# Attention and a feed-forward layer on one core: a new order of all queues and a new choice of engines for the same operations

## The chip, the cores and the metric

The kernel runs on one core of one Trainium2 chip. The metric is the device time in microseconds of one execution; the lower the better. The engines are TensorE (PE in the profile, its weight loads PEld), VectorE (DVE), ScalarE (ACT), GpSimd (POOL) and SyncE (SP), on whose queue all DMAs are issued.

## What is computed

The reference, cut to what matters:

```python
# q, k, v: (4, 12, 448, 64); w_in: (768, 2048); w_out: (2048, 768)
scores = cap * tanh(q @ k.T / 8 / cap)
attn = exp(scores - max(scores)); attn = attn / (sum(attn) + 1e-9)
x = (attn @ v) as (4 * 448, 768)
r = maximum(x @ w_in, 0)
out = (s * r * r + b) @ w_out
```

The weights come as 64-bit floats.

## The kernel before

The kernel does not run loops in the order in which they are written. A `Plan` first records 2446 operations, each with a number (its place in the recording), the engines that it may run on, and what it reads and writes. Then `emit` walks through the list `ORDER` (lines 120 and following), word by word. A word is an operation's number; a letter behind it chooses the engine, `a` for ScalarE, `d` for DVE, `p` for POOL, and none the first that the operation names. The words of one engine in their order are that engine's queue. Buffers come from pools with a fixed number of slots (`SLOTS`), given out in the order of the list, so the list also sets which operation waits for which buffer. Nothing else sets the order.

The work goes through these stages, which the list weaves together:

- Attention, for each of 4 batches `bb` and 6 pairs of heads `c2`: `load` and `loadv` bring operands; `plain` and `tail` (lines 426 and 432) are float32 products for the scores; `tanh` and `exp` (lines 441 and 445) run on ScalarE over 128x896 values; `add` on DVE or POOL sums the exponentials; `value`, `ends` and `total` (lines 496, 505, 536) are the products with v and with ones. `evac` and `evacs` (lines 479 and 545 on DVE) bring the results out of PSUM, `normal` turns the sums into reciprocals and spreads them through DRAM, `norm` multiplies.
- The weights. Each tile of w_in and w_out arrives as 64-bit floats and is turned into float32 by `last` (DVE, line 636), `expo` (ScalarE, line 641) and `join` (DVE, line 645); w_in is squared (`sq`, line 679 on DVE) for a norm, w_out summed (`csum`). Then each is split into two float16 halves, `_hi` and `_lo` (lines 341 to 343 and 360).
- `x` is split the same way (`x_hi`, `x_lo`).
- The first layer: `m1` for batches 0 and 1, with 448 columns (lines 828 to 830), and for batches 2 and 3 `m1p`, seven products of half size (line 969) that `plus` (DVE, line 931) joins; the products of the second kind use sums of weights, which `qfull`, `qsums`, `q_hi` and `q_lo` (lines 798 to 812) make, `saveq` stores in DRAM (`wq`, line 815) and `loadq` (line 943) reads back, three tiles for a pair of column groups.
- `relu`, `gsq`, `g_hi`, `g_lo`, `less`, `e_hi`, `e_lo`: the square and its two halves, and sums of them.
- The second layer: `m2` for batch 0 (lines 1140 to 1142), and `m2p` for batches 1 to 3, seven products of 224 columns in two halves each (line 1056), joined by `plus`. `load2` and `loadd` read the weights.

The numbers that the text below speaks of:

| number | operation | engine before, after |
|---|---|---|
| 797, 798 | expo and join of w_in tile (0,0) | ScalarE, DVE in both |
| 818, 819 | expo and join of tile (1,1) | ScalarE, DVE |
| 870, 871 | expo and join of tile (3,2) | ScalarE, DVE |
| 1681, 1645 | e_lo of batch 1, groups 7 and 5 | DVE |
| 1375 | qfull of tile (2,1) | POOL before, DVE after |
| 1391, 1392, 1393 | qsums, q_hi and q_lo of tile (3,1) | DVE, ScalarE; q_lo on DVE before, POOL after |
| 318 | tail of batch 1, pairs 4 and 5: the product that waits for the load of pair 5 | TensorE |
| 1394 | saveq of tile (3,1) | SP |
| 1838, 1839, 1840 | loadq of pair 1 for batch 2 | SP |
| 1753, 1754 | loadd of batch 1, pair 2 | SP |
| 1845 | m1p, batch 2, group 2, product 2: the first that needs pair 1's sums | TensorE |

Of the kernel before, what the change touches and what calls it, by code (L numbers as in the profile page):

```python
# [109 lines left out]
FAST = (1, 2, 3)  # L110
LEVEL = (0, 3, 3, 3)
SPLIT = ()
QUICK = (2, 3)
# [10 lines left out]
76 74 72 77 842 862d 822 75 190 819 824 78 815d 85 825d 89 137 820p 54d 826 57 849 853 86 872d 864 90 84 844 118  # L124
889 58 189 894 854 91 92 134 60 843 850 59 827 100d 122 96 87 851p 97 46 845 855 865 856d 123 119 47 846d 98 93
828 135 890 866 138 857 124 896 99d 94 829 867d 891 895 125 109d 873 874 128 61p 875 832d 131 136 876 126 102
129 127 101 905 111 0 892 834d 881d 48 882 906 887d 121 110 305 49 193 143 112 885d 140 910 150 897 144 139 132
151 130 888 145 133 899 194 141 113 877d 886 146 195 838d 142 191 147 199 196 878 883d 879d 148 830d 907 912 911
893d 200 941 197 149 201 152 202 833 103 908 913 155d 203 915 898p 205 104 153 208 164d 198 914d 836d 62 204 901
916 839 192 247 211 206 880 209 106 221d 50 214 207 884 215 154d 909d 216 900 902 217 218 105 249 166 210 222d  # L130
# [12 lines left out]
993 994 984 837 1432 995 998 508 999 1085 977d 509 985 417 990 986 1000 996 505 991 453 456 1001 461 1404a 1087
1003p 440 1090 462 246 982 469d 463 418a 358 421 420 506 1410a 1411p 1092 997 454 992 457 1451 1002 464 349 1412
1413 429 470d 499 514 458 1452d 1478 465 430 1077 1004d 987 1453p 1086 455 431 507 1414 500 1433 589 466 432 467
1078 468 472d 1091 360 1080 502 978 515 603 1008 477a 471d 1009 473d 587 510 503 1010 359 1484 1479 1485 474d
600 1081 1088 1082 1019a 475 1025a 1083 350 1093 1480 1500 1026 1005d 501 504 498 604 520 1095d 1023a 361p 521
1084 1089 295 1481 1021d 303d 601 422 1094 1024 522 1482d 1405d 476a 486a 1415 488 511 434 527d 1015a 517 1016
487 1096p 1006 1454 362 1416d 1017a 351 1013a 1486 605 512 1424 423 433 516 528d 1007 304 352p 1425 1011a 1434a
425 513 1079 1417p 353 1455 1100 1435d 1014 1101 1020 1102 1012 1111d 1022 1426 518 591 606 1112 1018 1117d  # L150
1113d 489 523 1115p 1487 478 519 607 1483d 1107a 1118 237 1114 524 525 535a 1103a 530d 1108 479 424 1427 526
1177 1466 1456 1104 1097d 1116 435d 1109a 1110 1178 531d 592 1490 529d 1436 490 532d 544a 363 1167 1169 1437
1179 480 1168 1428a 1488a 1172 1491 533 593 1438 1457 1439 1182 1458a 594 597 1173 590 1098 1180 645 588 1429p
1181 1174 1492 1184 598 534d 1440a 1493 1170 1183 1171 1175 1467 1187d 1105a 364 595 1185 1176 1418 608 1099
1419 1489p 596 1186 365 599 1442 1459d 1192 1188d 1193 1194 546 1443 1472 1106 1205a 481 602 1441d 436 1473 619d
1420 1460 1203a 536 537 1206 1421 647 1207a 1189d 538 1209a 482 620d 1514 1208 1210 1474 1494a 1195a 609 1444
1204 655 612 372a 370d 613 1201d 1495d 614 622d 1468 1197a 610 1120 1199d 1196 1198 1190 1202 373 368d 1131 492
1461 656 611 426d 661 1445 664 1200 1446a 369 371 615 646 491 366d 539 374a 1469 623d 616 1422a 662 627a 621d
617 483 618 624d 625 1133 1423d 1191 484d 1126 1132 1447d 1121 1027 1496 367 541 665 378 1127 1134 1497 1462 545
547 1128 663 375 1212 648 636d 1470a 1528 1122 626a 1119 493d 1123 1124 637 1129 494 1471p 1463 1464a 657 1136  # L160
638 548 649 650 652 653 1138 1141p 540 376a 1475 1135 1130 1125 1137 667 1465d 651 666 1476a 1139 658 1142p 1140
1146 427 703 705 1524 542p 1510 639 1143d 654 659 1147 680d 640 1511 1148 628 677d 660 543 629 1477d 550 1155a
1156 1149a 1151a 1150 1152 641 1512 1153a 1154 485 630 549 1157p 1525 1158 1161a 1159a 670 1163a 668 669 671
1286 672 710 707 1160 678d 1498 1211 1034 1499 679d 1039 631 1029 1035 1162 377 1041 681d 1164 1036 708 711 1513
1526 642 1030 632 1028 682d 1031 576d 643d 1040 1501a 1037 1515a 1032 1044 1042 704 1046 1521 1043 1038 683 1213
719 712 1049p 1045 1047 684a 1166 709 696 1033 1048 556p 686 633 1215 1165 1054 1055 673 1050p 674 1214 675 1056
676 1061a 1063a 687 720 1051d 735d 713 722 1059a 685a 1057a 1062 1064 634d 694a 1060 695 1216 714 1144 1058 1218
1217 1527 725 1223 715 635 1069p 1145 1071a 688 551d 697 723 1067p 552 721 553 736d 706 1072 698 724 716 1219
1070 717 1220 1228 689 700 1068 1073 738d 1259 728 1517 1518 726 718 1224 1221 727 1519 737d 1230 1225 739d 740d
1065a 741 699 1226 1229 690 691 729 730 1066 1231 742a 1233d 1227 731 1222 701p 1260 1232 732 744 745 1238 1234p  # L170
733 734 743a 1507 754 1261 753 746 1239 1520 644 702 755 1560 692p 1240 1249a 1262 747 1251a 752a 566d 1253a
1247a 1241a 756 749 748 1235d 1250 758 1255a 1252 1522a 1561 1248 1242 554 1243a 1556 1245a 1562 1236 757 1256
1557 1254 1244 750d 1538 1263 1273 1563 759d 1539 1313 1246 1264 1558 1529a 1074 1559 555 1265 1540 1503 1237
1266 1542 760 1690 764p 693 1535 1564p 1258 1530 1276 1267 1268d 1543 1270 1271d 1541 1277 1274 1290 1544 1531
1546d 1052 1592 1567a 1269 1257 1545 1565a 1278 1275 1279 1283 1568d 1566d 1053 1280 1284d 1281d 1547a 1287
1569d 1291 1292 1285 1610 1593 1300 1532 1502 1303 1282 1614 1288 1289 1548d 1293 1570d 1549a 1594 1297 1551d
1571d 1550d 1298d 1572a 1611 1294 1596 1272 1301 1595 1552d 1573d 1295d 1504 1327 1597 1302 1317 1533 1304 1600d
1603a 1612 1574 1598 1305 1599 1553d 1601a 1578 1296 1575 1613 1306 1307 1314 1604d 1615 1602d 1618d 1299 1579
1308d 1505 1506 1310 1554a 1605d 1311d 1318 1315 1616 1555d 1606d 1628 1319 1576 1316 1577 1715 1330 1629 1580
1582d 1581 1320 1534 1583a 1617 1682 1585a 1321 1619a 1324 1584d 1621a 1586d 1587d 1607d 1608a 1322d 1328 1523  # L180
# [51 lines left out]
def attention_moe_kernel(  # L232
# [1048 lines left out]
```

## Time and profile before

| what | us |
|---|---|
| median of 3 runs | 605.57 |
| lowest and highest | 604.0, 606.81 |
| the profiled execution's own time | 606.2 |
| its span, first to last instruction | 604.0 |

One execution of the kernel was recorded by the hardware profiler. Busy time of an engine is the time in which one of its instructions runs; issuing DMAs does not count. Matmuls are pipelined, so a matmul's own duration is longer than the step to the next, and a busy TensorE need not run at its full pace. In the views below an idle time in brackets stands before the instruction that ended it, with what released it.

### The profile page before, as it was taken

Reading aid. Unit: us, or ns where it says so; the run is one execution under the profiler, and the core shown is the slowest. Engines: PE = TensorE matmul, PEld = TensorE weight load, DVE = VectorE, ACT = ScalarE, POOL = GpSimd, SP = SyncE. Lnnn points to the kernel's source line nnn. Section 1 sums busy time; section 2 is a strip of 40 time slices with the busy share of each in tenths; the row PEclk is TensorE's granted clock in tenths of the full one; section 3 lists DMA queues with packets and bytes.
Section 4 is the critical chain, followed back from the end, with each engine's and each line's share of the span. In section 5 each row is a group of like instructions: output and inputs, shape, how many; then the busy total and the mean of one; then the engine's idle time right before and its main releaser. Section 6 shows DMA issues by size and latency. Waiting matters only on the chain.

```text
span 604.0 us, 12457 instructions
## 1 busy us (share of the span) xinstructions
PE 585.6 (97%) x4871; PEld 385.2 (64%) x4871; DVE 504.8 (84%) x1007; ACT 388.9 (64%) x570; POOL 121.9 (20%) x122
## 2 busy tenths in 40 slices
PE   5999999999999999999999999897999999999997
PEld 2332332343444444435555589897999999999997
DVE  1599999999999999999999999998889663577622
ACT  6999989998977997766869673133776114255100
POOL 0034013003211030411000010215242503363200
PEclk9999999999999999999999999998999999999999
DMA  8777665482435466565576787777575556563671
GB/s 322 293 223 256 172 219 167 113 300 71 113 112 184 141 234 219 167 221 184 211 231 237 239 303 248 263 253 260 183 269 208 186 187 198 178 223 137 248 258 62
DMA packets 56698, 125.24 MB, mean 207 GB/s; under 512 B 12736, under 2 KB 28224, under 8 KB 56640
## 3 DMA queue, kind: packets, MB, share of 16 engines
q1 hardware_dynamic: 56640, 124.45, 61.3%
q8 instruction: 38, 0.62, 0.4%
q14 instruction: 20, 0.16, 0.1%
HBM read 99.88 MB, written 24.47 MB: 206 GB/s over the span
## 4 chain that ended last, share of the span: by engine, by line
PE 62%; DVE 24%; ACT 6%; DMA 5%; issue 2%; SPq 0%; DVEq 0%; ACTq 0%
PE bank L1056 19%; PE bank L969 15%; DVE bed L349 7%; PE bank L829 4%; PE bank L828 4%; PE bank L830 4%; PE bank L496 3%; PE bank L426 3%; ACT bed L441 3%; DVE bed L645 2%; PE bank L1140 2%; PE bank L1142 2%; PE bank L1141 2%; DVE w L360 2%; ACT bed L445 2%
## 5 line engine op out<-in xcount | busy, mean ns | idle before, releaser
L349 DVE TENSOR_TENSOR bed<-bed 128x224 f32<-128x224 f32 (+6 forms) x193 | 150.4, 806 | 4.0 <-ACT bed L991 2.1
L1056 PEld LDWEIGHTS <-bed 128*128 128x128 f16 x1512 | 144.7, 98 | 3.5 <-issue 2.8
L350 POOL TENSOR_TENSOR bed<-bed 128x224 f32<-128x224 f32 (+4 forms) x71 | 71.3, 1018 | 291.0 <-DVE bed L349 88.7
L931 DVE SCALAR_TENSOR_TENSOR bed<-bank,arena,bed 128x224 f32<-128x224 f32 (+1 forms) x150 | 75.5, 525 | 63.4 <-PE bank L1056 26.2
L1056 PE MATMUL bank<-gt,bed 128*128 128x224 f16 x864 | 87.8, 259 | 2.5 <-DVE bed L931 2.5
L441 ACT ACTIVATE bed<-bank,arena 128x896 f32<-128x896 f32 x84 | 82.8, 1012 | 11.3 <-PE bank L426 3.9
L445 ACT ACTIVATE bed<-bed,par 128x896 f32<-128x896 f32 x84 | 85.4, 1049 | 0.1
L426 PE MATMUL bank<-bed 64*128 64x448 f32 x288 | 68.1, 584 | 6.7 <-DMA bed<-in_kq 5.0
L829 PE MATMUL bank<-bed,w 128*128 128x448 f16 x192 | 67.9, 353 | 0.0
L828 PE MATMUL bank<-bed,w 128*128 128x448 f16 x192 | 67.5, 351 | 0.0
L830 PE MATMUL bank<-bed,w 128*128 128x448 f16 x192 | 67.2, 350 | 0.0
L1056 PE MATMUL bank<-bed 128*128 128x224 f16 x648 | 66.8, 259 | 0.0
L969 PE MATMUL bank<-bed 128*128 128x224 f16 x576 | 60.9, 263 | 3.3 <-ACT gt L341 2.4
L496 PE MATMUL bank<-bed 128*32 128x448 f32 x576 | 62.2, 544 | 1.1 <-ACT bed L445 1.1
L969 PEld LDWEIGHTS <-bed 128*128 128x128 f16 x576 | 56.1, 99 | 4.8 <-ACT gt L341 2.6
L426 PEld LDWEIGHTS bank<-bed 64*128 64x128 f32 x288 | 24.9, 191 | 45.1 <-ACT bed L441 19.4
L969 PE MATMUL bank<-bed,w 128*128 128x224 f16 x432 | 45.8, 258 | 0.0
L360 DVE SCALAR_TENSOR_TENSOR bed<-bed,arena 128x256 f16<-128x256 f32 (+2 forms) x78 | 44.0, 594 | 0.0
L341 ACT ACTIVATE bed<-bed,arena 128x256 f16<-128x256 f32 (+2 forms) x56 | 30.9, 583 | 17.5 <-POOL bed L350 10.0
L969 PEld LDWEIGHTS <-w 128*128 128x128 f16 x432 | 41.4, 97 | 0.0
L496 PEld LDWEIGHTS bank<-bed 128*32 128x32 f32 x576 | 16.0, 109 | 39.2 <-issue 29.5
L988 ACT ACTIVATE bed<-bed 128x448 f32<-128x448 f32 x32 | 17.8, 568 | 36.1 <-DVE bed L931 36.0
(129 smaller groups left out, 801.7 us busy)
## 6 DMA issues: line engine op xcount, KB each, us to landing
bed<-ws SPq DMA_DIRECT2D x36, 512.0 KB, 4.6
bed<-w SPq DMA_DIRECT2D x30, 512.0 KB, 5.1
bed<-in_w_out SPq DMA_DIRECT2D x24, 512.0 KB, 4.2
bed<-wq SPq DMA_DIRECT2D x24, 512.0 KB, 4.5
bed<-in_kq SPq DMA_DIRECT2D x24, 448.0 KB, 4.4
bed<-in_w_in SPq DMA_DIRECT2D x18, 512.0 KB, 5.3
bed<-in_v SPq DMA_DIRECT2D x24, 256.0 KB, 4.7
w<-bed SPq DMA_DIRECT2D x12, 512.0 KB, 4.6
```

Source lines behind the costliest of these rows:

```text
L349: "DVE": lambda: nc.vector.tensor_tensor(dst(), a(), c(), op),
L350: "POOL": lambda: nc.gpsimd.tensor_tensor(dst(), a(), c(), op),
L426: nc.tensor.matmul(P[kp][:, h, 0:S], a[:, 0, c * 128:(c + 1) * 128], a[:, 1], start=True, stop=True)
L441: ("tanh", bb, c2, c), lambda: nc.scalar.activation(P[ke], P[kp][:, :, 0:S], AF.Tanh, scale=tsc[:, 0:1]),
L445: ("exp", bb, c2, c), lambda: nc.scalar.activation(P[ke], P[ke], AF.Exp, scale=par[:, 0:1]), r=["par"], w=[ke],
L496: nc.tensor.matmul(P[kp[x]][o, 0:S], P[kv[x]][:, c, o], P[kh[x][c]][:, h], start=not x and c == 0, stop=bool(x) and c == NC - 1,)
L828: nc.tensor.matmul(ps[:, 0:S], wh, x[:, 0], start=(c == 0), stop=False)
L829: nc.tensor.matmul(ps[:, 0:S], wh, x[:, 1], start=False, stop=False)
L830: nc.tensor.matmul(ps[:, 0:S], wl, x[:, 0], start=False, stop=(c == NP - 1))
L931: nc.vector.scalar_tensor_tensor(pick(to), ps, sc[:, 0:1], pick(of), ALU.mult, ALU.add)
L969: nc.tensor.matmul(at(), a(c, za), b(c, zb), start=c == 0 and n == 0, stop=c == NC3 - 1 and n == 2)
L1056: nc.tensor.matmul(at(), w(g, zw), b(g, zb), start=g == 0 and x == 0, stop=g == n - 1 and x == 2,)
```

## The change

Three lists are respelled without their spaces, which changes nothing, and `ORDER` is replaced as a whole. Of the 2446 operations 190 run on another engine; DVE has 836 operations in place of 833, ScalarE 573 in place of 569, POOL 106 in place of 113, TensorE (544) and SP (387) the same. The positions of nearly all words differ. The diff, cut to the lines that hold what the text speaks of:

```diff
-FAST = (1, 2, 3)
-LEVEL = (0, 3, 3, 3)
+FAST = (1,2,3)
+LEVEL = (0,3,3,3)
...
-QUICK = (2, 3)
+QUICK = (2,3)
...
 ORDER = """
-8 12 10 18 27 795 868 9 4 796 3 13 800 14 19 28 15 63 11 21 16 805 24 858 33 20 22 870 30 17 23 25 802 34 26 67
-35 2 36 29 797 65 5 806 801 811 40 798 847 816 64 799d 807 31 37 859 68 32 852 38 41 79 869 80 69 81 82 42 813
-83 871 848 818 808 860 809d 812 821 120 45d 70 863 43 39 88 71 95 803 73 44d 66 804p 56 55 823 814 810 817 861
...
-1342 1729 1697 1661p 1662a 1645d 1343d 559a 1749 1739 1743 1684 1663d 1681d 1740 560 568 1346 1344 1752 1355d
...
-763 1370d 1812 585 1392 575 1753 1775 1754 1776 1393d 1779 1359 1772 1781 1780 1764 1767 1770 1792 1813 1816
-1380p 1773 1381 1382 1371 1820 1786 1372 1383d 1814 1364 1379 1787 1788 1394 1790 1840 1815 1818 1838 1839 1789
-1822 1385p 1373p 1817 1791 1819 1793 1823 1843 1844 1821 1957 1384 1374 1796 1826 1395d 1827 1386 1845 1829a
...
+10 3 4 24 25 26 5 8 27 12 28 15 13 21 2 16 30 18 14 795 40 796 9 33 63 800 11 17 65 34 31 22 19 29 805 67 801
+847 20 868 32 806 811 64 70 23 76 41 42 812 35 77 71 869 6 68 120 72 816 69 43 44d 797 36 863 37 56 848 817 79
+38 55 73 66 88 78 80 74 81 798 852 82 39 821 818 118 819 57 83 89 54d 75 58 870 813 871 853 820d 814 807 85 95
...
+580 1679d 1644a 581d 1663d 1694 1730 1680a 1739 1684 1743 1681d 1645d 558 570 1737 1344 1731 1740 1729 561p 1687
...
+1391 1378d 1785 1764 1392 1792 1816 1788 1790 1787 1818 1813 1364 1815 1820 1359 1393p 1817 1844 1822 1794 1789
...
+1798 1394 1768 1771 1825 1383d 1840 1839 1772 1829a 1838 1753 1395d 1797 1769 1828p 1845 1767 1831a 1847 1830d
...
```

## Rows read from the trace of the kernel before

**Rows 1.** The page: each engine's busy time, share and instructions.

```profile
PE 585.6 (97%) x4871; PEld 385.2 (64%) x4871; DVE 504.8 (84%) x1007; ACT 388.9 (64%) x570; POOL 121.9 (20%) x122
```

**Rows 2.** Stretches: length, busy PE, PEld, DVE, ACT, POOL, granted clock, DMA share, GB/s.

```profile
0.00:20.00 20.00, 13.86 (x92) 4.60 (x96) 1.65 (x7) 14.51 (x18) 0.82 (x10) 1.00 0.89 343
20.00:380.00 360.00, 356.91 (x2574) 167.84 (x2565) 350.30 (x712) 296.03 (x415) 56.01 (x40) 1.00 0.62 201
380.00:425.00 45.00, 39.40 (x391) 37.95 (x389) 39.59 (x72) 13.99 (x20) 14.30 (x10) 0.96 0.73 246
425.00:604.00 179.00, 175.46 (x1828) 174.78 (x1825) 113.25 (x218) 64.34 (x119) 50.76 (x62) 1.00 0.56 195
```

**Rows 3.** The timeline: TensorE's last matmuls (start, length, engine, line).

```profile
598.21 2.46 PE L1056 MATMUL bank<-bed 128*128 128x224 f16 x24
```

**Rows 4.** The timeline of ScalarE and DVE in the first 24 us.

```profile
6.95 1.01 ACT L441 ACTIVATE bed<-bank,arena 128x896 f32<-128x896 f32 x1 [3.01 <-PE bank L426]
...
8.94 2.79 ACT L441 ACTIVATE bed<-bank,arena 128x896 f32<-128x896 f32 x3
...
19.17 1.29 ACT L641 ACTIVATE gt<-gt 128x512 f32<-128x512 f32 x2
...
19.91 0.69 DVE L645 SCALAR_TENSOR_TENSOR gt<-gt 128x512 int32<-128x512 int32 x1 [5.05 <-ACT gt L641]
```

**Rows 5.** DVE's groups by line: busy us, mean ns, idle time before.

```profile
L349 DVE TENSOR_TENSOR gt<-bed,gt 128x448 f16<-128x448 f32 x44 | 27.0, 631 | 0.7 <-POOL gt L343 0.6
...
L679 DVE TENSOR_TENSOR bed<-bed 128x512 bf16<-128x512 f32 x13 | 8.8, 682 | 0.1
...
L479 DVE COPY bed<-bank 128x448 f32<-128x448 f32 x13 | 7.9, 615 | 0.1
...
L545 DVE TENSOR_SCALAR bed<-bank,arena 128x448 f32<-128x448 f32 x7 | 4.7, 675 | 0.5 <-PE bank L536 0.5
```

**Rows 6.** POOL's groups by line and shape.

```profile
L350 POOL TENSOR_TENSOR bed<-bed 128x448 f32<-128x448 f32 x8 | 11.8, 1481 | 60.2 <-DMA bed<-zd 49.8 <-DMA bed<-in_v 10.5
L350 POOL TENSOR_TENSOR bed<-bed 128x512 f32<-128x512 f32 x7 | 10.9, 1559 | 45.9 <-DVE bed L645 32.3 <-DMA bed<-in_v 11.4 <-PE bank L426 2.2
...
L350 POOL TENSOR_TENSOR bed<-bed 128x1024 f16<-128x1024 f32 x1 | 2.1, 2134 | 0.0
```

**Rows 7.** DVE's and POOL's work on bed near 380.8 us (ns min/median/max), and POOL's timeline.

```profile
L349 DVE TENSOR_TENSOR bed<-bed x3: 385/1218/2309, 379.4 to 380.9; 128x224 f32<-128x224 f32 x2, 128x1024 f16<-128x1024 f32 x1
...
380.78 2.15 POOL L350 TENSOR_TENSOR bed<-w 128x1024 f32<-128x1024 f16 x1 [11.96 <-DMA bed<-w]
```

**Rows 8.** The chain that ended last, in order of time, and TensorE's timeline from 380 us.

```profile
74.91 4.87 DMA bed<-in_kq
...
385.79 2.46 PE L1056 MATMUL bank<-gt,bed 128*128 128x224 f16 x24 [2.05 <-DVE bed L931]
...
396.17 1.31 PE L1056 MATMUL bank<-gt,bed 128*128 128x224 f16 x12 [0.45 <-DVE bed L931]
...
417.15 0.45 PE L969 MATMUL bank<-bed 128*128 128x224 f16 x3 [2.39 <-ACT gt L341]
418.31 5.00 PE L969 MATMUL bank<-bed 128*128 128x224 f16 x33 [0.71 <-DMA bed<-wq]
```

**Rows 9.** Timelines of DVE, ScalarE and SP, and the chain, near 400 us.

```profile
397.76 0.42 DVE L807 TENSOR_TENSOR bed<-bed 128x256 f32<-128x256 f32 x1
...
403.04 1.22 DVE L349 TENSOR_TENSOR bed<-bed 128x1024 f16<-128x1024 f32 x1
...
401.30 1.05 ACT L810 ACTIVATE bed<-bed 128x1024 f16<-128x1024 f32 x1
...
400.72 3.89 SPq L815 DMA_DIRECT2D wq<-bed  x3
409.65 2.01 SPq L943 DMA_DIRECT2D bed<-wq  x3
...
411.27 6.99 DMA bed<-wq
```

More of the change, by code (lines that the diff above doesn't have):

```diff
@@ L126 @@
[L126 to L130, printed above, removed]
@@ new lines @@
+1207a 378 368a 1447d 620d 1496 622d 1206 1210 1462 1481 1463 611 1203a 1208 369 621d 590 1126 666 537 649 376a
+536 377 1429d 1131 538 650 370d 1482d 655 539 550 623d 615 1128 1492 703 616 1497 651 493d 1528 366a 484d 627a
+624d 656 1464a 1493 1133 652 661 372a 617 618 625 1132 1465d 374a 1494a 1121 1134 1127 670 1204 485 1129 1122
+626a 373 371 1123 541 1136 367 1124 638 629 540 637 1137 648 1130 1138 1141p 1125 705 1510 1139 1511 1483p 639
+1135 1512 662 1140 657 640 1146 556d 653 1142d 1495d 663 1498 636a 654 375 680d 1147 1513 1148 1499 677d 1190
@@ new lines @@
+1061d 1166 696 1527 686 695 706 1051d 737d 688 697 1059a 1057a 698 1064 1062 726 689 1229 1060 727 738d 1213
+1058 739d 1259 1220 1230 1071a 740d 1556 1065a 1215 1214 1072 699 741 1231 1223 729 576d 1221 1066 1069a 742a
+1144 1070 1519 1224 1216 730 691 700 1225 1226 690 745 1222 1145 744 731 1232 701d 746 754 1233p 753 1542 1227
+755 1073 1217 747 1067a 1234p 1235d 1238 756 1529a 743a 1239 1507 1068 1240 1241a 1243a 1245a 692d 1520 644 1260
+748 1247a 1242 554 555 749 1244 1246 1261 757 758 1255a 1249a 1251a 732 1248 733 750d 734 752a 1560 1263 1557
@@ new lines @@
+1252 1250 759d 1264 1074 1262 1256 1558 1265 1561 1503 1266 1559 1522a 1531 1253a 1313 1538 1273 1267 1270 1254
+1268d 1276 1562 1271d 1543 1052 1287 1277 1272 1258 1523 1274 1564d 1563 1565a 1544 1545 1278 1275 1279 1566d
+1567a 1568d 1547a 1290 1539 1280 1569d 1281d 751 1570d 1690 1540 1541 1283 1291 1535 1592 1593 1532 1596 693
+1546p 1282 1284d 1285 1594 1548p 1571p 1595 1597 1300 1288 1516 1303 702 1572a 1549a 1292 1598 1289 1551d 1269
+1257 1600d 1317 1293 1297 1294 1550d 1573d 1314 1236 1298d 1599 1295d 1552d 1304 1305 1578 1533 1504 1237 1603a
@@ new lines @@
+1897 1806p 1898 1860a 1807d 1863d 1389 2050 1397 1398d 1885 1808a 1809d 1901 1886 1883 1861d 1910 1884 1930
+1864p 1903 1865d 1866p 1904 1906 1905 1888a 1908 1907 1909 1867a 1932 1987 1868p 1911 1913 1916 1399 1929 1914
+1889d 1931 1956 1917 1938 1936 1887p 1892d 1890a 1915 1891p 1958 1934 1933 1919a 1940 1935 1937 1893p 1939 1774
+2019 1894d 1967 1997 1918d 1895d 1921p 1941 1920d 1896d 1960 1942 1943 1944 784d 1995 1923d 1961 1963 1962 1965
+1922d 1964 1969 1924p 1971 1945 1966 1925d 765a 1926a 764d 1968 586 1970 1989 1947a 1778 2048 1991 1927d 1988
@@ new lines @@
+1972 1948d 2018 1990 2023 1992 787d 2051 1973 1993 1946d 2060 1974 1994 2066 1999 1975 774d 1949a 1976 1977d
+1980a 1950p 1996 2056 2015 767d 1981d 2069 1998 2001 1978a 2000 2002 766 1951d 1714 2003 2016 788 1952d 2005d
+785a 2024 2004 768 2008d 2049 2006a 2037 2020 1710 2034 2009d 2007d 2028 2070 2053 2010d 2011d 2025 2026 2027
+1979d 2052 2057 2012d 2013a 1982p 775d 1953d 777d 786 2061 778 2114 2014d 2058 2021 2031 2038 1983d 1984d 1985p
+2059 1954a 2143 2022 2062 1955p 1986d 2029 769d 2144 770p 2063 2054 2064 2072 2065 2067 2035 2030 776 2040 779p
@@ L227 @@
+2344p 2384 2406 2392 2395 2399 2374 2286p 2287a 2351 2354 2364 2345d 2402 2346p 2288p 2413 2347p 2365 2355 2414
[3 rows of a table added]
 """
```

162 lines of the change are left out of this document (71 added, 91 removed), and 6 rows, old and new, of the table ORDER.

## The prediction

> **What bounds the kernel now.** The page comes first: TensorE is busy for 585.6 of 604.0 us [rows 1], so a new order of the same work can win little more than what TensorE idles, 18.4 us, and the part of its busy time in which matmuls stand drawn out. The table of engines by stretch comes next [rows 2]; the reader is to see three stages in it. From 20 to 380 us DVE is busy for 350.3 of 360 us, idle 9.7: whatever DVE has queued before the second products sets the end of that stage, and TensorE, though shown busy, runs drawn out (2574 matmuls in 360 us). From 380 to 425 us both have gaps: TensorE 5.6 us, DVE 5.4. From 425 us TensorE is bound by its own work: 1828 matmuls in 175.46 us, 0.096 each, whatever their inputs do; its missing 3.5 us there lie almost wholly behind its last matmul, which ends at 600.67 [rows 3]. DVE is idle there for 66 us. So the end is: DVE's start, plus DVE's work up to the products, plus what is lost from 380 to 425 us, plus some 179 us that no order shortens.
>
> **The change, part by part.** The first two edits only take spaces out of two tuples and cost nothing; the third replaces the list of operations. No operation is added or removed.
>
> *The start of DVE's work.* DVE stands idle until 19.91 us but for some 1.65 us of small work [rows 2, 4], because the first join (798) waits for ScalarE's rescaling of weight tile (0,0) (797): "5.05 <-ACT gt L641". On ScalarE that is the 16th activation in the old list, the 21st in the new one, behind the constant and 19 tanh or exp of 128x896. ScalarE starts them at 6.95 us and three take 2.79 us, each starting some 0.9 after the one before [rows 4], so 797 would start at about 6.95 + 19 x 0.9 = 24.1, and the join 0.74 behind it, as from 19.17 to 19.91 today, at 24.8: 4.9 us later. DVE's next join (819) waits for 818, four exp or tanh further (some 29), and the one behind it (871) for 870, two further (some 31.5); between these two joins DVE has only two short steps. From there its queue has its inputs in hand. So DVE loses between 4.9 us, if the later waits are made good by TensorE having other work, and 7, if each counts whole. I take 5.5, near the single wait that is certain.
>
> *Work moved between DVE, ScalarE and POOL.* Ahead of the last split of j=1 that TensorE waits for (1681 in the old list, 1645 in the new), I counted both lists by kind. DVE loses four evacuations of 0.615, two of 0.675, three squares of 0.682 [rows 5], two column sums, two x_hi and one x_lo, and gains six normalisations (448 columns, near 0.63 by the subtraction of that width in rows 5), three lesx and some single steps: about 3 us less. TensorE has one block of 12 matmuls (1.15 us) less queued ahead of the matching products. Net, DVE comes to this point some 2 us earlier against TensorE. The six evacuations and three squares go to ScalarE, some 6 us by their times on DVE, and a good part of them before 120 us, where ScalarE is as full as DVE. What covers it is that exp and tanh stand earlier against TensorE's products in the new list, and if that cover fails up to 3 us come back; that is in the range.
>
> *POOL.* Ahead of the same point POOL has 34 operations, not 38: six fewer normalisations (1.48 each), two more column sums (1.56), the rest near even [rows 6], some 6 us less. It matters since DVE is drawn out beside POOL: a subtraction of 128x224 that otherwise takes 0.385 took 2.309 us while POOL ran 2.15 us from 380.78 [rows 7]. The bounds are 0 (POOL's operations mostly hit no DVE work) and 6 (each blocks DVE throughout). As DVE has little idle time with 56 us of POOL beside it [rows 2], most do not block: I take 1. That very pair is also gone: the sum on POOL (1375) is DVE's in the new list.
>
> The first stage together: + 5.5 - 2 - 1 = 2.5 later, less about 1 for what TensorE waited for from 75 to 80 us (the load of the scores' operands, 4.87 us [rows 8]), which moves from SP's 70th place to the 67th while the product that waits for it, 318, moves from TensorE's 88th to the 91st; it is partly hidden today behind DVE. So 1.5 us later; the bounds run from -4 (POOL whole, start half hidden) to +6 (start whole, nothing given back).
>
> *From 380 to 425 us.* TensorE idles 2.05, 0.45, 2.39 and 0.71 us, and then 33 matmuls take 5.00 us [rows 8]: at 0.096 each 3.2 would do, so 1.8 more is lost. The granted clock of this window has a mean of 0.96 [rows 2], so part of it ran at 1.2 instead of 2.4 GHz, just after the idle time. Together 7.4 us. The first two gaps wait for DVE's additions, one of them behind the 2.309 us step; I leave 1.2 of 2.5. The last three are one chain: q_lo of tile (3,1) runs on DVE at 403.04 [rows 9], 5 us after the last of its sums (397.76 to 398.18); its save is SP's third, whose issue ends at 404.61; the loads of pair 1 stand behind in SP's queue, at 409.65, and land until 411.27 + 6.99 = 418.26. So 14 us lie between the end of q_lo and its last landing. In the new list q_lo (1393) is on POOL directly behind its sums and ScalarE's copy: 1.05 on ScalarE [rows 9], then 2.13 on POOL by the row of the same size [rows 6], some 3.2 us after the sums, not 6.1. Queued behind the save on SP are the pair's three loads and loadd; the product that needs them (1845) has six blocks of m2p(1,2) of 1.15 us moved in ahead of it, though the work that 380 us finds done is smaller in turn, so I count no more than 0.5 for this. The chain gives back 2.9 + 0.5 of its 4.9: 1.5 remain, 2.7 with the first two gaps. So -4.7; the bounds are -7.4 and 0.
>
> *The rest.* From 425 us the new list has DVE, ScalarE and POOL in other orders, but DVE is idle for 66 of 179 us; nothing there comes to bear. A stall would cost its own length.
>
> *Sum.* 1.5 - 4.7 = -3.2 us on a span of 604.0. That profiled execution took 606.2 us, the runs shown 604.0 to 606.81 with a median of 605.57; taken off the median, 602.4.
>
> **The rivals.** *Slower: the late start is carried through.* DVE has 9.7 us of idle time in 360, too little to catch up. If the 5.5 us stay whole, the 2 us and POOL's 1 are eaten by ScalarE's added 6 us, and 1393's chain, now behind POOL, is late by as much as DVE, then no gap at 380 to 425 us closes: 605.6 + 5.5 = 611. It decides once DVE's first join is over 5 us later and the idle of TensorE from 380 to 425 us is still over 5. For it: the row of the wait at 19.91; against: the work moved off DVE.
>
> *No change:* the loads of pair 1 still take 14 us from q_lo, so that only 2.5 us of the gaps are saved, and the first stage is 2.5 late: 605.6.
>
> *Faster by more: POOL blocks DVE as a rule.* The 2.309 us step shows one subtraction held for as long as POOL's. If most of POOL's 6 us were such, the first stage would be 5 us earlier than in my sum at the most; with 3.5 of it, 602.4 - 3.5 = 598.9. The Trainium skill (SBUF — State Buffer, "Who interferes with whom") has the pair of ports that the two engines share as an exclusive lock for a whole instruction, where whichever issues first blocks the other; by that rule the whole 6 us could come. The trace agrees in the step named, and its 350.3 us of busy DVE do not tell how many others there are.
>
> **How the numbers follow.** The likeliest is my sum, 602.4, between 599.5 and 605.5, with 0.42: half of that, 0.21, lies under 602.5. Faster by more 0.26, no change 0.12, slower 0.20. A measurement of this kernel tells about 0.5% from no change, 3 us: 602.5 and 608.6. Faster by over 0.5%: 0.21 + 0.26 = 0.47; within: 0.21 + 0.12 = 0.33; slower: 0.20. The range goes from 595 (the sum with both stages near their good bounds) to 609.5 (part of the slower case); it leaves out some 0.06 below and 0.14 above.
>
> **What would show it.** Right: DVE's first L645 starts near 25 us, not 19.9; DVE stays full until some 380 us; TensorE's idle time from 380 to 425 us falls under 3 us and the clock stays at 1.00; POOL's long sum no longer stands beside a stretched DVE step. Wrong: TensorE again waits for wq or DVE's additions at 380 to 425 us, new waits for loads show up elsewhere, or DVE's idle time after 40 us grows.

## The result, and the profile after

| | before | after |
|---|---|---|
| median of 6 runs each, same chip | 605.97 us | 598.59 us |
| lowest and highest | 603.66, 607.44 | 597.73, 599.16 |
| span of the profiled execution | 604.0 us | 597.0 us |

The ratio is 0.9883, with a 95% interval of 0.9859 to 0.9907: 7.1 us faster, between 5.6 and 8.5. The forecast was 602.4 with a range of 595.0 to 609.5 and "faster" as the likeliest sign; the time lies in the range, 3.8 us under the forecast.

The page's first part of the new kernel, against [rows 1]:

```profile
PE 583.7 (98%) x4871; PEld 385.6 (65%) x4871; DVE 492.2 (82%) x1010; ACT 390.0 (65%) x574; POOL 112.5 (19%) x115
```

The table by stretch of the new kernel, to be laid beside [rows 2] (length, busy PE, PEld, DVE, ACT, POOL, granted clock, DMA share, GB/s):

```profile
0.00:20.00 20.00, 14.95 (x86) 5.60 (x90) 1.68 (x6) 14.14 (x16) 1.34 (x11) 1.00 0.69 248
20.00:40.00 20.00, 20.00 (x180) 5.66 (x176) 11.56 (x23) 19.91 (x25) 0.00 (x0) 1.00 0.88 300
...
20.00:380.00 360.00, 355.15 (x2567) 167.12 (x2560) 342.73 (x711) 299.98 (x424) 47.03 (x36) 1.00 0.63 207
...
360.00:380.00 20.00, 17.56 (x167) 16.68 (x165) 19.80 (x33) 4.55 (x6) 5.73 (x4) 0.91 0.77 263
...
380.00:425.00 45.00, 44.98 (x472) 44.82 (x470) 42.57 (x83) 19.58 (x30) 16.56 (x12) 1.00 0.73 256
425.00:604.00 179.00, 168.60 (x1758) 168.11 (x1755) 105.20 (x212) 56.32 (x106) 47.54 (x57) 1.00 0.56 192
```

And two stretches of the kernel before that were not shown yet:

```profile
20.00:40.00 20.00, 19.83 (x184) 6.37 (x178) 18.64 (x36) 20.00 (x26) 4.66 (x3) 1.00 0.79 270
...
360.00:380.00 20.00, 20.00 (x210) 19.77 (x208) 19.48 (x35) 7.16 (x11) 2.53 (x4) 1.00 0.83 288
```

Read three things. DVE's late start is there: 11.56 us of work from 20 to 40 us against 18.64. The idle time of TensorE from 380 to 425 us is gone: 44.98 of 45 busy and 472 matmuls instead of 391, at a clock of 1.00 instead of 0.96. But a part of it stands earlier now: from 360 to 380 us TensorE idles 2.44 us and the mean granted clock falls to 0.91, where the old kernel had no gap. From 425 us TensorE takes 168.60 / 1758 = 0.096 us a matmul, as before.

Where does one stage end and the next begin? A mark that both lists have is the end of the last split of j=1 (e_lo) on DVE. DVE's timeline, first of the old, then of the new kernel (start, length, engine, line; the step is the last of three in each row):

```profile
364.02 2.75 DVE L349 TENSOR_TENSOR bed<-bed 128x1024 f16<-128x1024 f32 x3
```

```profile
360.83 2.41 DVE L349 TENSOR_TENSOR bed<-bed 128x672 f16<-128x672 f32 x3
```

It ends at 366.77 and 363.24: the first stage is **3.5 us earlier**. From there to the end of the span it is 237.2 and 233.8, so the rest gave **3.4 us**. The forecast had + 1.5 and - 4.7 us. The end itself, TensorE's last matmuls in the new kernel against [rows 3]:

```profile
591.28 2.46 PE L1056 MATMUL bank<-bed 128*128 128x224 f16 x24
```

They end at 593.74, against 600.67; 3.3 us lie behind them in both. So the sign of the first stage was wrong, and three questions were left for runs: is the late start really a loss, if that stage came out earlier; what paid for it; and was it the engine of q_lo(3,1) that closed the gaps behind 400 us.

Two measures are used below. **DVE's lag** at a time is the start of the last step that began before it, less the usual lengths of all steps queued ahead (the time from one start to the next, where DVE does not wait): all that it has lost so far to waits and to steps drawn out. A wait that is still running at that time is not in it yet. **Drawn-out steps** are DVE's steps before 360 us that took over 0.25 us more than the usual length of their kind; 0.1 us of each is not counted. Worked out from the traces, not rows of a view:

```
                        DVE's lag (us)   drawn-out steps   last split     span less
                        at 40  at 360    us      number    of j=1 ends    that end
before                  21.6   38.1      9.1     19        366.8          237.2
after                   27.4   38.7      2.1      5        363.2          233.8
before_expo_late        26.7   45.6     11.0     20        374.3          234.1
before_norm_dve         22.1   35.8      6.5     13        368.7          234.4
before_qlo_early        22.6   41.0     11.8     20        369.7          234.6
expo_early              32.8   46.2      2.1      5        370.8          233.8
after_norm_pool         27.2   44.3      8.9     13        364.7          232.2
after_qlo_dve           26.7   38.6      2.3      6        363.1          233.2
joins_first             26.4   41.1      2.3      6        365.7          232.2
after_engines_before    27.7   56.9     12.8     21        385.5          240.6
```

Every drawn-out step of the first two rows lies beside an operation of POOL. The lag shows one thing more: at 360 us it is nearly the same in both lists (38.1 and 38.7). DVE's larger loss at the start is offset by the end of the stage, and the 3.5 us that remain are work that its queue no longer holds ahead of the mark: by the usual lengths, its steps up to the last split come to 327.7 us in the old list and 324.1 in the new one. In the kernels of the experiments the same statements stand two lines lower (L645 is L647, L931 is L933).

### The profile page after: what moved, and what is told of

It reads as the page before. It is cut to its first block, busy times and chain, and to the rows that moved or that the text cites. A ratio compares the mean times of both kernels' runs of the same rounds, so it can differ in the third digit from the quotient of the medians.

```text
span 597.0 us, 12475 instructions
## 1 busy us (share of the span) xinstructions
PE 583.7 (98%) x4871; PEld 385.6 (65%) x4871; DVE 492.2 (82%) x1010; ACT 390.0 (65%) x574; POOL 112.5 (19%) x115
## 5 line engine op out<-in xcount | busy, mean ns | idle before, releaser
L349 DVE TENSOR_TENSOR bed<-bed 128x224 f32<-128x224 f32 (+6 forms) x199 | 147.7, 766 | 5.1 <-POOL gt L350 3.0
L350 POOL TENSOR_TENSOR bed<-bed 128x224 f32<-128x224 f32 (+5 forms) x65 | 71.2, 1106 | 284.6 <-DVE bed L645 93.1
L931 DVE SCALAR_TENSOR_TENSOR bed<-bank,arena,bed 128x224 f32<-128x224 f32 (+1 forms) x150 | 75.5, 524 | 55.7 <-PE bank L1056 20.7
L1056 PE MATMUL bank<-gt,bed 128*128 128x224 f16 x864 | 89.8, 261 | 2.4 <-DVE bed L931 2.4
L969 PE MATMUL bank<-bed,w 128*128 128x224 f16 x432 | 47.5, 260 | 0.0
```

Source lines behind the costliest of these rows:

```text
L349: "DVE": lambda: nc.vector.tensor_tensor(dst(), a(), c(), op),
L350: "POOL": lambda: nc.gpsimd.tensor_tensor(dst(), a(), c(), op),
L931: nc.vector.scalar_tensor_tensor(pick(to), ps, sc[:, 0:1], pick(of), ALU.mult, ALU.add)
L969: nc.tensor.matmul(at(), a(c, za), b(c, zb), start=c == 0 and n == 0, stop=c == NC3 - 1 and n == 2)
L1056: nc.tensor.matmul(at(), w(g, zw), b(g, zb), start=g == 0 and x == 0, stop=g == n - 1 and x == 2,)
```

## The experiments

All ratios are to the kernel before, run on the same chip as the experiment (its medians there were 606.4 to 607.1 us); the new kernel's is 0.9883, from the six runs above, so two ratios are compared and not two times.

### Four splices of the two lists: they tell of seams

start_before is the first 96 words of the old list and then all other words in the new list's order; start_after the first 138 of the new and then the old order; first_after and first_before cut at 1680 words of the new and 1600 of the old, near the end of the first stage.

```diff
 ORDER = """
-10 3 4 24 25 26 5 8 27 12 28 15 13 21 2 16 30 18 14 795
+8 12 10 18 27 795 868 9 4 796 3 13 800 14 19 28 15 63
...
```

> The first 96 words of the old list, then the new list's order for all the rest. Theory A (DVE sets the end of the first stage, so its later start costs, and the new list makes up for it elsewhere): the first join is back near 20 us and DVE keeps most of the 7 us, so 593 to 596 us, below the new kernel's 598.6. Theory B (the late start costs nothing, because TensorE and ScalarE set the first stage): 597.5 to 600 us, as the new kernel, with DVE idle for the time won.

> The first 138 words of the new list, then the old list's order for all the rest. Theory A: the late start is carried through the old list's first stage, 606 + 5 to 7 = 611 to 613 us. Theory B: 605 to 607.5 us, as the old kernel.

> The first 1680 words of the new list (until the first product of the third pair of batch 1, near 385 us), then the old list's order. If the two stages add, the first stage's 3 us are kept and the rest is lost: 602 to 604 us. If the stretch from 380 to 425 us owes its gain to the state in which the first stage leaves DVE, 598 to 600; if the new first stage only works with its own sequel, 606 or more.

> The first 1600 words of the old list (until near 362 us), then the new list's order. If the stages add: 606 - 4 = 601 to 603 us, with TensorE's idle time between 365 and 425 us at some 2.4 us and no wait for wq. If the gaps from 380 to 425 us come from DVE's lateness rather than from the order there, 605 to 607.

Measured: start_before 614.86 us, ratio 1.0132 [1.0092, 1.0172]; start_after 619.67, 1.0209 [1.0166, 1.0251]; first_after 607.9, 1.0020 [0.9993, 1.0047]; first_before 611.32, 1.0075 [1.0047, 1.0104]. All four are slower than the new list, three of them slower than the old one too; first_after can't be told from the old one. Of all the expected values only the third of first_after, 606 or more, was met. The stretch behind the seam, first of start_before with the wait of DVE and the one of ScalarE that end just behind it, then of start_after with TensorE's longest wait there:

```profile
20.00:40.00 20.00, 17.05 (x136) 4.45 (x128) 10.79 (x21) 16.45 (x20) 1.51 (x2) 0.91 0.58 209
...
42.05 0.75 DVE L647 SCALAR_TENSOR_TENSOR bed<-bed 128x512 int32<-128x512 int32 x1 [9.05 <-ACT bed L643]
...
40.42 1.01 ACT L443 ACTIVATE bed<-bank,arena 128x896 f32<-128x896 f32 x1 [3.37 <-PE bank L498]
```

```profile
40.00:60.00 20.00, 10.69 (x90) 4.03 (x86) 16.50 (x46) 10.54 (x15) 3.75 (x3) 0.66 0.33 109
...
PE bank L691 <- DVE bed L681: 7.0, 3, 3.2
```

In start_before the first join comes nearly as early as in the old list (20.58 us), but from 33 to 42 us DVE stands still: the rescaling that it waits for is queued on ScalarE behind a tanh that itself waits 3.37 us for a product. At 60 us DVE's lag is 34.3 us. In start_after TensorE is busy for 10.69 of 20 us, and for 7.0 us it waits for DVE's squares. The two later splices lose behind their seam too; TensorE's waits from 380 to 425 us in first_after are for loads alone:

```profile
PE bank L971 <- DMA bed<-wq: 4.0, 3, 1.9
...
PE bank L1058 <- DMA bed<-ws: 2.5, 1, 2.5
```

So these four do not tell the theories apart. What they show is that a stretch of such a list can't be priced by putting it in front of another list: it needs the inputs, loads and buffers that its own beginning leaves behind. The experiments that follow move a few operations within one list, or change engines alone.

### before_expo_late: the first term of the sum by itself

ScalarE's queue of the old list, from its 14th place; no other engine's queue changes:

```diff
-26 29 797 807 31 68 32 80 69 81
+26 29 807 31 68 32 80 69 797 81
```

> The old list with the first rescaling (797) alone moved to the 21st place (counted from 0) on ScalarE, behind the five activations that followed it; nothing else moves. It is the first term of my sum by itself: 797 starts 4.2 to 4.9 us later, the first join at 24.5 us. Theory 'DVE's late start is carried through to the end' (+5.5 in my sum): DVE is later by 4 to 5 us at 40 us and at 360 us, the time is 610 to 611 (a ratio of 1.007 to 1.009). Rival 'made good before 60 us': 606 to 607.5 (1.000 to 1.003).

Measured: 612.76 us, ratio 1.0097 [1.0062, 1.0132], **+ 5.9 us** (3.8 to 8.0). DVE's timeline:

```profile
26.18 0.71 DVE L647 SCALAR_TENSOR_TENSOR gt<-gt 128x512 int32<-128x512 int32 x1 [11.07 <-ACT gt L643]
```

The first join starts at 26.18 us, not 19.91 [rows 4], behind 11.07 us of idling; DVE's lag is 5.1 us larger at 40 us and 7.5 at 360 (1.9 of these in drawn-out steps). The late start is carried through. So the forecast's term of + 5.5 was sound, and "made good before 60 us" falls.

### expo_early: the opposite move in the new list

ScalarE's queue of the new list from its 15th place:

```diff
-32 23 77 71 68 72 69 797 78 80 74 81 818 83 75 870 813
+32 23 797 818 870 77 71 68 72 69 78 80 74 81 83 75 813
```

> The new list with three of ScalarE's rescalings alone moved up: 797, 818 and 870 stand 16th to 18th on ScalarE instead of 21st, 26th and 29th; all other queues and engines are as in the new list. In the new kernel the first join starts at 27.0 us, in the old one at 19.9. Theory 'the late start is paid in full behind the first stage' (the first step of my sum): the first join comes near 20.5 us, DVE's whole queue shifts by 5 us, and the time falls by 4 to 5, to 594 us, a ratio to the kernel before near 0.980. Rival 'DVE makes the start good later, since in the old kernel its early work only ran ahead of inputs': DVE's idle time after 30 us grows by as much, and the time stays at 598.6 +- 1.5, a ratio of 0.986 to 0.990; the tanh and exp behind the three come 2.5 us later, so a stall of TensorE before 60 us could even make it slower.

Measured: 607.59 us, ratio 1.0013 [0.9989, 1.0037]: 8 us **slower** than the new kernel, where 4 to 5 faster or the same was expected; a slowdown was named as possible, without a size. ScalarE's timeline, and TensorE's longest new wait:

```profile
24.20 0.70 ACT L643 ACTIVATE gt<-gt 128x512 f32<-128x512 f32 x1 [3.66 <-DMA gt<-in_w_in]
```

```profile
PE bank L507 <- ACT bed L443: 4.9, 1, 4.9
```

818 stood on ScalarE before its weight tile had landed; the tanh and exp behind it waited too, and TensorE for them. The same load is in the new kernel's own start, in DVE's timeline:

```profile
22.58 0.44 DVE L636 TENSOR_SCALAR gt<-gt 128x512 int32<-128x512 int32 x1 [4.10 <-DMA gt<-in_w_in]
...
26.66 0.43 DVE L636 TENSOR_SCALAR gt<-gt 128x512 int32<-128x512 int32 x1 [2.37 <-DMA gt<-in_w_in]
27.00 0.69 DVE L645 SCALAR_TENSOR_TENSOR gt<-gt 128x512 int32<-128x512 int32 x1
29.97 0.69 DVE L645 SCALAR_TENSOR_TENSOR gt<-gt 128x512 int32<-128x512 int32 x1 [2.27 <-ACT gt L641]
...
32.44 0.69 DVE L645 SCALAR_TENSOR_TENSOR bed<-bed 128x512 int32<-128x512 int32 x1 [1.18 <-ACT bed L641]
```

The first join starts at 27.00 us with no wait of its own, right behind a step that waited 2.37 us for a load: in the new list DVE's start is set by the landing of tile (1,1), not by 797, which ScalarE starts at 25.00. The run agrees with the theory that it was to test, from the other side, though it holds TensorE up as well: the lag that it has more than the new kernel at 40 us, 5.4, is 7.5 at 360 us, and the time is 8 us more.

### joins_first: fill the idle start with work that has its inputs

ScalarE's and DVE's queues of the new list:

```diff
-23 77 71 68 72 69 797 78 80 74 81 818 83 75 870 813 807 802 84
+23 797 802 807 77 71 68 72 69 78 80 74 81 818 83 75 870 813 84
...
-806 812 869 44 848 817 798 819 57 54 871 853 820 814 815 45 864 808 855 809 100 822 803 799 804 109
+806 798 799 803 804 808 809 812 869 44 848 817 819 57 54 871 853 820 814 815 45 864 855 100 822 109
```

> The new list with DVE's idle start filled: ScalarE's rescalings of weight tiles (0,0), (0,1) and (0,2) (797, 802, 807), whose loads have landed by 18 us, stand 16th to 18th instead of 21st, 32nd and 31st, and on DVE their joins and squares (798, 799, 803, 804, 808, 809) stand before the steps that wait for the loads of tiles (1,0) and (1,1) until 22.6 and 26.7 us. Other queues and all engines are as in the new list. Theory 'DVE's start is carried through': six steps of 0.69 us are done in time in which DVE stood idle, DVE is 3 to 4 us earlier at 40 us and at 360 us, and the time is 595 to 596 (a ratio to the kernel before of 0.981 to 0.984). Rival 'TensorE's early products are what the start waits for': the five activations that stand behind the three come 1.7 us later, DVE then waits for evacuations, and the time is 598 to 600 (0.987 to 0.990).

Measured: 600.09 us, ratio 0.9889 [0.9864, 0.9914]: no gain. DVE's timeline begins as meant and then idles later:

```profile
21.05 0.70 DVE L647 SCALAR_TENSOR_TENSOR gt<-gt 128x512 int32<-128x512 int32 x1 [2.65 <-ACT gt L643]
...
31.27 0.70 DVE L647 SCALAR_TENSOR_TENSOR gt<-gt 128x512 int32<-128x512 int32 x1 [3.89 <-ACT gt L643]
...
41.06 0.62 DVE L481 COPY bed<-bank 128x448 f32<-128x448 f32 x1 [1.19 <-PE bank L498]
```

The six steps are done by 25.1 us, but the next join waits 3.89 us for ScalarE instead of 2.27, and from 20 to 40 us TensorE is busy for 18.86 us with 158 matmuls (new kernel: 20.00 and 180). DVE's lag is 1.0 smaller than the new kernel's by its last step before 40 us, but there it stands in a wait for a product that ends at 41.06; at 60 us the lag is 1.6 larger. ScalarE is full in that stretch of the new kernel (19.91 of 20), so what DVE gets early there, TensorE gets late. The time falls where the second theory put it: DVE's start hangs on ScalarE's and TensorE's as well, and the new list's start is not improved by this.

### after_norm_pool and before_norm_dve: what an operation on POOL costs DVE

The new list with the eight normalisations that it took off POOL put back, and the old list with the same eight on DVE:

```diff
-61d 116d 245d 361d 352d 542d 701d 692d
+61p 116p 245p 361p 352p 542p 701p 692p
```

> The new list with one change: the eight normalisations that it took from POOL to DVE are back on POOL, at the same places in the order. On DVE they are 8 x 0.63 = 5.0 us, on POOL 8 x 1.48 = 11.8 by the rows of before. By 'POOL's whole time blocks DVE': DVE is later by 11.8 - 5.0 = 6.8 us and the time near 605 (0.999). By the share that the old trace shows, 9.1 us of drawn-out DVE steps beside 56 us of POOL, 1.9 us of blocking against 5.0 of work saved: DVE is 3 us earlier, the time 595.5 (0.983), unless their 0.85 us of later results cost TensorE a wait each. By 'neither counts': 598.6 (0.988). I expect the middle for DVE's drawn-out steps (4 us instead of 2) and a time of 597 to 600.

> The old list with the eight normalisations that the new list took off POOL on DVE, at their places. DVE has 8 x 0.63 = 5.0 us more to do, POOL 11.8 less. Theory 'a normalisation on POOL draws DVE out by as much as it would take there' (in the new list the eight on POOL drew DVE's steps out by 6.8 us more, and the time stayed): DVE's drawn-out steps fall from 9.1 to 3 or 4 us, the time stays, 606 +- 1.5 (a ratio of 0.998 to 1.002). Rival 'POOL blocks DVE only by the share seen in the old trace, 9.1 of 56 us': 3 us slower, 609.5 (1.005).

Measured: after_norm_pool 599.55 us, ratio 0.9875 [0.9826, 0.9924]; before_norm_dve 606.3 us, 0.9994 [0.9969, 1.0020]. **Neither move changes the time** by more than its interval (3 us either way for the first, 1.6 for the second), though each shifts 5 us of DVE's work. The first interval just takes in the 0.983 that the old trace's share gave, so there the trace has to decide. In after_norm_pool every one of the eight draws out one step of DVE: drawn-out time 8.9 us instead of 2.1, so 6.8 us more for 5.0 saved. That is far above that share of POOL's time (1.9) and below the whole of it (11.8); its last split comes 1.4 us later. Three of the places in POOL's timeline of after_norm_pool:

```profile
47.05 1.15 POOL L352 TENSOR_TENSOR bed<-bed 128x448 f32<-128x448 f32 x1 [45.00 <-DMA bed<-zd]
...
156.88 1.14 POOL L352 TENSOR_TENSOR bed<-bed 128x448 f32<-128x448 f32 x1
...
224.86 1.14 POOL L352 TENSOR_TENSOR bed<-bed 128x448 f32<-128x448 f32 x1
```

and in DVE's:

```profile
47.27 0.96 DVE L701 TENSOR_SCALAR arena<-arena 128x2 f32<-128x2 f32 x1
...
156.92 1.65 DVE L647 SCALAR_TENSOR_TENSOR bed<-bed 128x512 int32<-128x512 int32 x1
...
224.04 1.23 DVE L367 TENSOR_REDUCE arena<-bed 128x2 f32<-128x512 f32 x2
225.30 0.73 DVE L763 TENSOR_TENSOR arena<-arena 128x8 f32<-128x8 f32 x1
```

The same join in the new kernel, where nothing runs on POOL beside it:

```profile
156.57 0.68 DVE L645 SCALAR_TENSOR_TENSOR bed<-bed 128x512 int32<-128x512 int32 x1
```

The join of after_norm_pool at 156.92 begins 0.04 us behind POOL's step and takes 0.97 us more. The step of two columns at 47.27 ends at 48.23, 0.03 us behind POOL's (48.20), and the one of eight columns at 226.03, again 0.03 behind POOL's (226.00): DVE's instruction stands until POOL's has ended. The two reductions at 224.04, beside which POOL's steps ran too, keep their 0.62 us each. The Trainium skill ("SBUF — State Buffer", section "Who interferes with whom") says which these are: an instruction of DVE with two inputs in SBUF, or one in a mode that uses both ports, is shut out for the whole of a POOL instruction that was first and reads SBUF, and a reduction never is. The trace agrees in these rows, the reductions included; whether the step of two columns ran in such a mode it does not tell.

In before_norm_dve the drawn-out time falls from 9.1 to 6.5 us only, and still the time stays. The old list's steps are drawn out by a varying amount (9.1, 10.9, 11.0 and 11.8 us in four executions that have the eight on POOL), so the run sets 5.0 us more work against some 4 us less of that, which fits a time that stays. The rival's 1.005 is outside the interval. (The 10.9 is first_before's, whose list is the old one to the end of the first stage.)

### after_engines_before: the new order with the old engines

All 190 operations back on their engine of before, at the new places:

```diff
-820d 804d 851d 61d 155a 840d 914p 893p 116d
+820p 804p 851p 61p 155d 840a 914d 893d 116p
...
```

> The order of the new list, but all 190 operations that changed their engine are put back on their engine of before (POOL 122 operations again). Theory 'the choice of engines makes the gain, by less of POOL beside DVE and by 1393 on POOL': DVE's drawn-out steps before 360 us come back from 2 us to 6 or 9, the wait for the loads of pair 1 comes back, and the time is 604 us or more (a ratio of 0.997 or above). Rival 'the order of the queues makes it': no more than 2 us over the new kernel, 599 to 600.5 (0.988 to 0.991).

Measured: 628.0 us, ratio 1.0336 [1.0280, 1.0391]. The rival (599 to 600.5) falls; the first theory said 604 or more and named nothing that would make it 24 us more. The wait for the loads of pair 1, expected back, did not come. The stage from 20 to 380 us, against 355.15 busy TensorE with 2567 matmuls, 342.73 DVE and 47.03 POOL in the new kernel:

```profile
20.00:380.00 360.00, 340.52 (x2379) 149.17 (x2372) 335.86 (x677) 291.79 (x410) 63.12 (x37) 1.00 0.58 191
```

POOL has 63 us there; drawn-out steps come back from 2.1 to 12.8 us, over the 6 to 9 expected, and DVE's lag at 360 us is 18.2 us larger. Some 11 of these 18 are steps held by POOL; the other 7 are gaps of DVE's, waits that no run here splits further. So the new order alone is not the gain: with the old engines it puts POOL into DVE's way. But as the two work together in this list, the run does not say how much of the 7 us either is worth.

### after_qlo_dve and before_qlo_early: the chain of the loads of pair 1

The new list with q_lo(3,1) on DVE (1393p to 1393d), and the old list with ScalarE's copy one place up and q_lo four places up on DVE:

```diff
-1842 1392 1382
+1392 1842 1382
...
-1391 1378 763 1370 585 575 1393 1764
+1391 1378 1393 763 1370 585 575 1764
```

> The new list with q_lo of tile (3,1) (1393) on DVE again, at its place in the order, not on POOL. Theory 'its engine is what brings the loads of pair 1 forward': on DVE it waits for ScalarE's copy and stands before or behind some DVE steps, its save and the loads move by 1 us or more, and the time is 599.5 to 601.5 (0.990 to 0.993). Rival 'the place in the order did it (the sums and the copy come earlier), the engine is indifferent': 598.6 +- 1 (0.987 to 0.990), with the loads of pair 1 landing within 1 us of the new kernel's.

> The old list with the chain of the loads of pair 1 alone brought forward: ScalarE's copy 1392 stands before the snapshot 1842 (which waited 4.24 us for a product) instead of behind it, and q_lo 1393 directly behind the sums of tile (2,1) on DVE; engines as before. Theory 'this chain sets the stalls at 411 to 419 us' (most of the -4.7 of my sum): q_lo starts near 399.5 instead of 403.0, the save and the three loads move 3.5 us, TensorE's gaps of 2.39 and 0.71 us close, and the time falls by 2.5 to 4 us: 602.5 to 604 (a ratio of 0.993 to 0.996). Rival 'the loads are late for another reason (their places and buffers), or DVE's additions behind are now later by the 1.2 us of q_lo': within 1 us of before (0.998 to 1.002).

Measured: after_qlo_dve 598.46 us, ratio 0.9857 [0.9809, 0.9905]; before_qlo_early 605.65 us, 0.9986 [0.9966, 1.0006]. **The engine makes no difference** that the runs can tell. Here is q_lo, first in after_qlo_dve, then in the new kernel:

```profile
399.65 1.22 DVE L351 TENSOR_TENSOR bed<-bed 128x1024 f16<-128x1024 f32 x1
```

```profile
397.74 2.13 POOL L350 TENSOR_TENSOR bed<-bed 128x1024 f16<-128x1024 f32 x1 [9.65 <-ACT bed L810]
```

It starts 1.9 us later on DVE and ends 1.0 later; by the traces the last of the three loads lands at 409.4 us instead of 409.0, and no wait for them comes back. The expected 2.5 to 4 us in the old list did not come either; the interval allows 2.1. Why the old chain was late stands in ScalarE's timeline of the kernel before, ahead of the copy of [rows 9]:

```profile
400.76 0.63 ACT L979 ACTIVATE bed<-bank,arena 128x448 f32<-128x448 f32 x1 [4.24 <-PE bank L969]
```

The copy stood behind a snapshot that waited 4.24 us for a product; in the new list it starts at 396.61 instead of 401.30:

```profile
396.61 1.06 ACT L810 ACTIVATE bed<-bed 128x1024 f16<-128x1024 f32 x1 [2.46 <-PE bank L969]
```

TensorE's timeline in before_qlo_early:

```profile
388.69 3.38 PE L1058 MATMUL bank<-gt,bed 128*128 128x224 f16 x24 [2.19 <-DVE bed L933]
391.86 2.10 PE L1058 MATMUL bank<-bed 128*128 128x224 f16 x12
...
410.29 6.20 PE L971 MATMUL bank<-bed 128*128 128x224 f16 x63 [0.20 <-DVE bed L933]
416.88 1.02 PE L971 MATMUL bank<-bed 128*128 128x224 f16 x9 [0.39 <-DVE bed L933]
```

and SP's:

```profile
401.46 3.71 SPq L945 DMA_DIRECT2D bed<-wq  x2
405.27 2.28 SPq L817 DMA_DIRECT2D wq<-bed  x3
411.85 5.82 SPq L945 DMA_DIRECT2D bed<-wq  x4
```

The waits of 2.39 and 0.71 us of [rows 8] are gone, but two things had a part in it that are not the edit's: this execution came to the stage 2.9 us later than the one in the rows, though its queues are the same up to 397 us, and it lost 1.7 more right at its first gap, where 24 and 12 matmuls take 3.38 and 2.10 us (2.46 and 1.31 in other rows) while the mean granted clock from 390 to 400 us is 0.83, between the two levels of 1.2 and 2.4 GHz. q_lo starts at 402.92 us, not at the 399.5 expected. The loads of pair 1 stand at 411.85, 2.2 us later than in the rows: with TensorE 4.6 later behind that gap, that closes the wait. On SP the saves stood behind a load issue of the pair before (401.46, two in 3.71 us), so copy and q_lo came early to a queue that was blocked by something else. How much of the 2.4 us that the loads won on TensorE is the edit's, the run does not tell.

This also corrects how the first profile is to be read. In the three other traces of the old list with an unbroken order, each with an edit of its own, the time from the last split to the end of the span is 234.1 to 234.6 us, not 237.2. A likely reading is that a first stage that ends later has fewer stalls behind it, since the loads keep their own pace; no run tests it, and in the new list expo_early's first stage ends 7.6 us later with the same 233.8 behind it. The five traces of the new list that keep its engines but for those named have 232.2 to 233.8. So by these traces the new list wins 0.3 to 2.4 us behind the last split, not 3.4, and the larger part of its 7 us ahead of it: 366.8, 368.7 and 369.7 in the old list (without the late start), 363.1, 363.2 and 364.7 in the new one.

## Why the prediction was right or wrong

The time came out inside the range and faster, as forecast, but not by the sum: - 3.2 us were forecast and 7.1 measured, the first stage had the wrong sign, and the stage that was to bring the whole gain brought half of it at the most. That the range held is in part luck.

**DVE's late start, + 5.5.** Right in size: before_expo_late gives + 5.9 by itself, and the lag at 40 us grew from 21.6 to 27.4. The first join's time was forecast as 24.8 and was 27.0, because it was priced by ScalarE's queue alone; the wait for tile (1,1) on DVE's own queue was not seen. The second and third joins came at 29.97 and 32.44, as worked out (some 29 and 31.5, plus 0.74).

**Work moved off DVE, - 2, and POOL, - 1.** Here the forecast failed. The step was: "The bounds are 0 ... and 6 ... As DVE has little idle time with 56 us of POOL beside it [rows 2], most do not block: I take 1." Most of POOL's time did not block, but 19 steps were held, 9.1 us in all; in the new list 5 are, 2.1 in all. So by the traces this term was - 7, not - 1. It lies beyond the bound of 6, which counted only what POOL has less to do: in the new list what stays on POOL holds DVE less as well (2.1 of its 47.0 us, against 9.1 of 56.0). And normalisations moved to DVE were booked as work added there, although in after_norm_pool each of the eight holds DVE by 0.85 us on average from POOL (6.8 / 8), where on DVE it takes 0.63. The term for the work was too small too: the forecast counted about 3 us less on DVE and took 1 of them off again for TensorE's block, and the steps up to the last split come to 3.6 us less. With - 7 and - 3.6 in their places, + 5.8 for the start and nothing for the loads, the sum is - 4.8; the profile pair shows - 3.5, and the 1.3 us between them are further waits of DVE's that no run splits. The three traces of each list named above lie 4.7 us apart in the mean (368.4 and 363.7). The forecast's lower bound for this stage, - 4, does not follow from its own terms either: half the start (2.7), the work (2), POOL whole (6) and the load (1) give some - 6.

This account is drawn from the traces, step by step; no run takes the gain back by one part. The eight normalisations change nothing in either list, and no run moves the evacuations and squares that went to ScalarE by themselves. What the runs do show is the price of the late start and that POOL holds DVE.

**The load of the scores' operands, - 1.** Wrong: TensorE's longest wait of the new kernel is that one, and the list of waits of the kernel before has the same line:

```profile
PE bank L426 <- DMA bed<-in_kq: 5.0, 1, 5.0
```

**From 380 to 425 us, - 4.7.** What was seen there came true: no gap, clock 1.00. But the stall moved as much as it went. TensorE's timeline of the new kernel:

```profile
375.21 3.74 PE L1056 MATMUL bank<-gt,bed 128*128 128x224 f16 x24 [2.44 <-DVE bed L931]
```

2.44 us of waiting for DVE's additions, and 24 matmuls in 3.74 us instead of 2.46: 3.7 us, half of the old 7.4, are lost just ahead of the stretch that the sum looked at. Of the cause named, q_lo's engine and its place behind its sums, the engine made no difference (after_qlo_dve), and the place alone brought no gain in the old list (before_qlo_early); and by the other traces the stall that it was to close was partly one of that single execution. The profile pair's - 3.4 has the sign of the term; the other traces say 0.3 to 2.4 us.

**The rest, 0.** Right: from 425 us TensorE's pace is 0.096 us a matmul in both.

**The rivals.** "The late start is carried through" is a true mechanism with the right price, but its condition failed: the gaps closed, and less work on DVE and fewer held steps paid for the start. "POOL blocks DVE as a rule" gave 598.9, and 598.59 was measured; its mechanism is the one that the normalisation runs show, so it deserved more than 0.26. That it meets the time to 0.3 us is luck all the same: it kept the - 4.7 of the second stage, and the pair gave - 3.4 there. Its condition was in reach: the drawn-out steps of the old trace could have been counted ahead of the prediction, where one was taken as an example.

No kernel tried here is measurably faster than the new one: after_qlo_dve's ratio (0.9857) and after_norm_pool's (0.9875) lie within each other's intervals and that of the new kernel.

## What to carry to other kernels

Where two engines hold each other up, price an operation on the lesser one by what it holds the bound engine, step by step in the trace, before it is called free: here a normalisation that takes DVE 0.63 us held it for 0.85 from POOL. A loss at the start of the engine that bounds a stage came out whole at the end here (before_expo_late), but before moving its first inputs forward look at every queue that they pass: each of three engines' queues, and the loads, set the same start in turn. And a gap in one profiled execution is a sample: compare the same stretch in several traces before it is priced, and do not cut a list in two to price its halves.

## What the runs showed of the hardware that was not expected

An instruction of DVE on 8 columns took 0.73 us and one on 2 columns 0.96 because each stood until POOL's had ended; so short steps are held as long as large ones. Two traces with the same queues up to 397 us (before and before_qlo_early) differed by 2.9 us in DVE's lag at 360 us, and by 2.7 in drawn-out steps: which of DVE's steps an operation of POOL holds is not settled by the queues alone. And behind 425 us, where TensorE alone is the bound, DVE's steps of before_qlo_early and of the kernel before stay 0.29 to 0.31 us apart from 432 us to the end, and those of before_norm_dve 0.91 to 0.93, each but for one step: what differs between these executions arose in the stages ahead.
